# Three PSUM tiles for the attention results, routing constants on GpSimd, and a new instruction order, in an attention and mixture-of-experts kernel

## The chip, the cores and the metric

The kernel runs on one core of a Trainium2 chip. The metric is the device time of one execution in microseconds (us), here the median of several runs. The engines are named as the profile names them: PE is TensorE's matmul, PEld its weight load, DVE is VectorE, ACT is ScalarE, POOL is GpSimd and SP is SyncE, which issues most DMAs.

## The reference

Inputs q, k, v have 8 batches, 8 heads, 576 positions and 64 channels. The first half is attention with a memory:

```
scores = q k^T / 8, causal;  a = softmax(scores);  local = a v
q_p = phi(q),  phi(x) = x + 1 for x > 0, else exp(x)
mem = (q_p M_prev) / (q_p z_prev + 1e-6)
out = sigmoid(beta) * mem + (1 - sigmoid(beta)) * local
```

The second half takes the 4608 positions as tokens x of 512 channels. Logits are x times w_gate, for 8 experts. Pairs of token and expert are taken in the order of falling logits, with at most 576 tokens for an expert. Each expert e then computes relu(x w1[e]) w2[e] for its tokens.

## The kernel before

Values are kept as pairs of 16-bit floats (a high part and a rest), so that the products are nearly of 32-bit accuracy. Attention is done in 16 units of four heads (a unit is half of a batch). For each unit the kernel loads q, k, v and M_prev, splits and transposes them, takes row maxima of the scores, and then, head by head, makes the scores in PSUM (`S`), exponentiates them on ACT into a high part `ph` and a full value, and subtracts the two into a low part `pl` (`P2`: on DVE at line 1339 or on POOL at line 1342, as a letter of the string `p2k` says for each of the 12 pieces of a unit).

With these a head's results are made on PE. A row of queries has five blocks of positions. `AVm` is 10 matmuls that make the five blocks of memory results, `AV1`, `AV2` and `AV3` are 9, 21 and 15 matmuls that make the five blocks of local results. Every result block has 65 columns: 64 channels and the denominator. Each matmul of these is recorded at line 1041, a helper. All blocks of all heads lie in one PSUM tile of three banks:

```
avs=ps.tile([128,3,512],F32,name='avs')
def slot(i): return avs[:,2*b,65*i:65*i+65] if i<7 else avs[:,1,65*(3*b+i-7):65*(3*b+i-6)]
```

`b` is 0 or 1 and alternates from head to head: a head has bank 0 or bank 2 for seven blocks, and three places in bank 1, the middle bank, for the rest. On DVE a head then takes `N0` (two instructions, lines 1385 and 1386, that gather the denominators), `N1` (reciprocal, line 1390), `N2` (line 1389, the memory blocks divided, out of PSUM into the SBUF tile `xt`; two instructions, as the blocks lie in two banks), `N2b` (line 1389, the local blocks divided in place, in PSUM) and `N3` (line 1403, their sum into `xt`). Three of four heads go so; the fourth divides all ten blocks in one step and leaves the sum to POOL. The results are then split into 16-bit pairs (`ncast`, `nsub`), written to DRAM and multiplied with w_gate into logits.

After attention the kernel routes: for each of 8 experts a threshold is searched on DVE, ACT and PE, the tokens' numbers are listed, the rows gathered, and two matrix products run. All but the first expert's routing lies beside the products of the expert before.

The order is planned by a program in the kernel file. Each of its nodes has an engine, or alternatives, a duration, data keys that it reads and writes, pools of buffers that it takes (`acq`) and frees (`rel`), and a due time; a list schedule follows from these. The table `PR` holds the due times' offsets (`off`, `dl`), additions to durations that steer the choice between engines (`bias`), fixed choices by piece (`pin`, where `*` leaves it free) and `p2k`. The planner treats the two halves of `avs` as two independent buffers (`av=2`). The instructions are then issued in that order, and the waits between engines are made from the tiles that the instructions touch.

Constants for routing are made during attention (`route_consts`, lines 1498 to 1506 on DVE, after integer patterns from POOL), and the gate weights are scaled and split at the start (line 1152, three instructions on DVE).

Of the kernel before, what the change touches and what calls it, by code (L numbers as in the profile page):

```python
# [23 lines left out]
          'kba': -30628.42,  # L24
          'kbd': -21514.39,
          'kbv': -30457.33,
          'kha': -9689.05,
          'khp': 68039.52,
          'khv': 14252.18,
          'klp': -32138.21,  # L30
          'klv': -19015.13,
          'mh2a': 18046.34,
          'mh2v': -7557.72,
          'mha': -6556.62,
          'mhv': 118047.29,
          'mlp': -61301.72,
          'mlv': 103205.55,
          'mra': 13094.26,
          'mrv': -49929.19,
          'mza': 13667.92,  # L40
          'mzv': 154718.09,
          'nap': -923.34,
          'nav': -3267.9,
          'nca': -17356.34,
          'ncp': 19952.5,
          'ncv': -19147.84,
          'nsp': -33806.3,
          'nsv': 8700.47,
          'p2p': 3448.83,
          'p2v': -5.41,  # L50
          'p4sp': -99613.75,
          'p4sv': -14317.61,
          'pha': -24715.3,
          'php': 10489.25,
          'phra': -10695.76,
          'phrv': 20287.52,
          'phv': -24278.1,
          'plp': 4297.99,
          'plv': 4879.76,
          'prepca': -46562.05,  # L60
          'prepcv': -134550.89,
          'qha': -51241.95,
          'qhp': 17974.64,
          'qhv': -60171.16,
          'qlp': 26287.18,
          'qlv': 78420.0,
          'qmovea': 42586.74,
          'qmoved': 5914.55,
          'qmovev': -9885.0,
          'tea': -3123.88,  # L70
          'tev': -3783.25,
          'vha': -3050.15,
          'vhp': 15722.78,
          'vhv': 48350.7,
          'vlp': 27996.84,
          'vlv': 29979.61,
          'xtea': -62406.89,
          'xtev': 142184.48},
 'dl': {'0': {'AV': 3.03,
              'MX': -439.58,  # L80
              'N': -45.87,
              'P2': 95.25,
              'S': -79.48,
              'fin1': 396.93,
              'fin2': 87.35,
              'kb': 3.48,
              'kh': -937.23,
              'kl': -795.9,
              'kt': 387.88,
              'lk': -688.72,  # L90
              'lm': -210.42,
              'lq': -541.06,
              'lv': -99.14,
              'maxrem': -157.75,
              'mfin': 328.48,
              'mfin2': -56.76,
              'mfin3': -180.29,
              'mh': -838.83,
              'ml': 193.21,
              'mz': -1034.64,  # L100
              'nadd': -286.28,
              'ncast': 852.81,
              'nsub': -703.35,
              'ph': -141.8,
              'phe': -764.62,
              'phr': -38.36,
              'phs': 62.7,
              'pl': -977.2,
              'prep': 200.37,
              'proc24': 671.37,  # L110
              'pt': 192.37,
              'qh': -404.47,
              'ql': 386.07,
              'qmove': 129.64,
              'qt': -168.61,
              'sj4': -1434.02,
              'vh': 667.29,
              'vl': 490.09},
        '1': {'AV': 58.78,
              'MX': -104.28,  # L120
              'N': -347.1,
              'P2': -339.06,
              'S': 606.52,
              'fin1': 484.59,
              'fin2': 2.45,
              'kb': 126.23,
              'kh': -563.06,
              'kl': 507.8,
              'kt': 591.73,
              'lk': -540.92,  # L130
              'lm': -577.58,
              'lq': -166.76,
              'lv': -66.59,
              'maxrem': 342.62,
              'mfin': -545.34,
              'mfin2': 9.06,
              'mfin3': -80.01,
              'mh': -618.46,
              'ml': 449.29,
              'mz': 14.48,  # L140
              'nadd': -926.32,
              'ncast': -198.57,
              'nsub': 506.43,
              'ph': -560.71,
              'phe': -372.41,
              'phr': -876.37,
              'phs': 209.62,
              'pl': 213.14,
              'prep': 164.36,
              'proc24': 454.72,  # L150
              'pt': 233.41,
              'qh': -427.92,
              'ql': 1274.93,
              'qmove': 1075.02,
              'qt': 47.11,
              'sj4': -45.54,
              'vh': -285.68,
              'vl': -176.11},
        '10': {'AV': 758.58,
               'MX': -73.66,  # L160
               'N': 72.38,
               'P2': 279.63,
               'S': -8.46,
               'fin1': -248.92,
               'fin2': 347.06,
               'kb': 358.91,
               'kh': 442.41,
               'kl': 79.29,
               'kt': -298.24,
               'lk': -767.97,  # L170
               'lm': 14.63,
               'lq': -633.6,
               'lv': 673.6,
               'maxrem': 724.62,
               'mfin': -318.66,
               'mfin2': 386.87,
               'mfin3': 137.35,
               'mh': 981.75,
               'ml': -129.7,
               'mz': 550.95,  # L180
               'nadd': -120.05,
               'ncast': 1.51,
               'nsub': -229.44,
               'ph': 489.25,
               'phe': 997.89,
               'phr': -1284.21,
               'phs': 165.79,
               'pl': -224.45,
               'prep': 191.53,
               'proc24': -144.35,  # L190
               'pt': -242.79,
               'qh': 501.96,
               'ql': 984.38,
               'qmove': -284.76,
               'qt': -711.9,
               'sj4': -187.91,
               'vh': 1156.16,
               'vl': -17.9},
        '11': {'AV': 355.99,
               'MX': -108.14,  # L200
               'N': -177.3,
               'P2': -1118.12,
               'S': 356.14,
               'fin1': 358.76,
               'fin2': 223.29,
               'kb': -146.64,
               'kh': -152.48,
               'kl': 559.23,
               'kt': -15.25,
               'lk': 955.17,  # L210
               'lm': 246.97,
               'lq': 882.81,
               'lv': -420.65,
               'maxrem': 30.53,
               'mfin': -41.22,
               'mfin2': 83.89,
               'mfin3': -400.44,
               'mh': -51.28,
               'ml': -126.76,
               'mz': -129.3,  # L220
               'nadd': 107.08,
               'ncast': -1366.45,
               'nsub': 536.08,
               'ph': -283.95,
               'phe': -649.23,
               'phr': -270.74,
               'phs': -481.4,
               'pl': 292.58,
               'prep': -518.41,
               'proc24': -4.05,  # L230
               'pt': -249.01,
               'qh': 480.34,
               'ql': 615.5,
               'qmove': 459.89,
               'qt': -26.77,
               'sj4': 164.57,
               'vh': -414.34,
               'vl': 21.65},
        '12': {'AV': 167.39,
               'MX': 1.03,  # L240
               'N': 559.11,
               'P2': -154.37,
               'S': -49.69,
               'fin1': 221.57,
               'fin2': 527.79,
               'kb': 1200.71,
               'kh': -74.53,
               'kl': -144.63,
               'kt': -309.14,
               'lk': -221.84,  # L250
               'lm': -263.39,
               'lq': -614.17,
               'lv': 244.4,
               'maxrem': 565.59,
               'mfin': 257.23,
               'mfin2': 16.16,
               'mfin3': 507.27,
               'mh': 215.36,
               'ml': 291.75,
               'mz': 463.51,  # L260
               'nadd': -356.78,
               'ncast': 12.76,
               'nsub': 868.62,
# [631 lines left out]
class Sched:  # L895
# [18 lines left out]
    def run(self,tol=100,sem=170,same=110,t0=0.0,hwg=450,dlat=1300,dend=950,ph=2800.0,thr=3060,pel=60):  # L914
# [20 lines left out]
        def pick(e):  # L935
            C=cand[e]; best=None; L=[]; Q=line[e]
            f=free[e]
            for c in C:
# [7 lines left out]
                elif e=='V' and (x.slack or x.nm in LK) and s<poolb-1: s=poolb-1  # L946
# [11 lines left out]
        while left:  # L958
            b=None
# [931 lines left out]
```

## Time and profile before

| | us |
|---|---|
| median of 3 runs (971.52 to 975.38) | 972.42 |
| profiled execution | 974.23 |
| span of its instructions | 972.40 |
| busy: PE / DVE / POOL / ACT | 814.7 / 717.4 / 599.7 / 578.3 |
| mean granted TensorE clock (1.0 is 2.4 GHz) | 0.947 |

The profiled execution is 1.8 us above the median and its span 1.8 us below its time. Busy time is summed over stages that have different limits, so it is read stage by stage: attention takes about the first 495 us, the routing of the first expert with nothing beside it about 60 us, and the experts the rest.

### The profile page before, as it was taken

What the parts mean: (1) busy time and instruction counts of PE and PEld (TensorE: products, weight loads), DVE (VectorE), ACT (ScalarE), POOL (GpSimd) and SP (SyncE); (2) the same over time, 40 slices, a digit from 0 to 9 for tenths busy, and PEclk for the clock granted to TensorE, in tenths of its full rate; (3) what the DMA queues carried; (4) which work ended last, traced back from release to release, by engine and by line L of the source; (5) the groups of instructions that cost most, each with busy time, mean ns of one, the idle gap of its engine ahead of it and who ended that gap; (6) DMA issues with size and microseconds to landing.
All of it is one profiled execution on the core that took longest, in us unless ns stands there. A gap on an engine that the chain in (4) does not pass through costs nothing.

```text
span 972.4 us, 25309 instructions
## 1 busy us (share of the span) xinstructions
PE 814.7 (84%) x9736; PEld 523.4 (54%) x9736; DVE 717.4 (74%) x2385; ACT 578.3 (59%) x1046; POOL 599.7 (62%) x594
## 2 busy tenths in 40 slices
PE   4587888878888888888831797999999999999995
PEld 3365666656667666767620543445454444444442
DVE  8998889998889899896678977768787777502010
ACT  4475776677587767768622557483838383754110
POOL 7768787889889878968610237382647373585101
PEclk9897999999899999999955699899999999999999
DMA  5566454528555443533411427362737273692101
GB/s 130 117 142 147 111 118 93 128 66 168 115 131 124 92 105 69 118 66 66 94 36 61 162 79 220 127 177 81 231 102 237 94 232 102 216 269 78 38 12 38
DMA packets 230302, 116.49 MB, mean 120 GB/s; under 512 B 199013, under 2 KB 208229, under 8 KB 230181
## 3 DMA queue, kind: packets, MB, share of 16 engines
q1 hardware_dynamic: 224293, 96.00, 39.1%
q0 software_dynamic: 5888, 18.88, 5.8%
q8 instruction: 76, 1.25, 0.5%
q14 instruction: 45, 0.37, 0.1%
HBM read 72.40 MB, written 18.87 MB: 94 GB/s over the span
## 4 chain that ended last, share of the span: by engine, by line
PE 44%; DVE 7%; issue 1%; ACT 1%; DMA 1%; POOL 0%; POOLq 0%; DVEq 0%; ACTq 0%
PE py L1540 19%; PE ph L1540 16%; PE avs L1041 3%; PE prem L1540 2%; DVE scr L1774 2%; PE pr L1540 1%; DMA out_dram<-ys,idx 1%; PE pb L1041 1%; DVE xt L1389 1%; PE pl L1540 1%; DVE avs L1389 1%; DVE xt L1403 0%; DVE th L1781 0%; ACT wh L1689 0%; DVE kk L1780 0%
## 5 line engine op out<-in xcount | busy, mean ns | idle before, releaser
L1690 POOL TENSOR_TENSOR wl<-wst,wh 128x1024 f16<-128x1024 f32 x60 | 127.6, 2150 | 81.9 <-ACT wh L1689 64.7
L1540 PE MATMUL ph<-xT,wh 128*128 128x512 f16 (+1 forms) x560 | 164.0, 368 | 1.7 <-DVE hl L1733 1.0
L1334 ACT ACTIVATE ph<-pb 128x512 f16<-128x512 f32 x192 | 115.7, 602 | 42.5 <-PE pb L1041 32.0
L1197 DVE TENSOR_REDUCE mx<-pb 128x1 f32<-128x512 f32 (+3 forms) x256 | 123.3, 547 | 2.2 <-PE pb L1041 2.0
L1041 PE MATMUL avs<-V,ph 128*128 128x65 f16 x1792 | 103.6, 194 | 24.8 <-DVE xt L1389 11.4
L1752 POOL DMA_INDIRECT out_dram<-ys,idx x40 | 38.7, 968 | 126.3 <-ACT ys L1747 70.9
L1041 PEld LDWEIGHTS <-ph 128*128 128x128 f16 x1792 | 94.3, 99 | 33.4 <-issue 30.3
L1342 POOL TENSOR_TENSOR pl<-pf,ph 128x512 f16<-128x512 f32 x80 | 95.2, 1193 | 19.7 <-ACT pf L1341 18.3
L1041 PE MATMUL pb<-qT,kT 128*128 128x64 f16 (+3 forms) x576 | 102.3, 242 | 6.0 <-DVE mx L1197 2.8
L1540 PEld LDWEIGHTS <-wh 128*128 128x128 f16 x1072 | 68.7, 99 | 59.3 <-issue 3.8
L1041 PE MATMUL avs<-V,pl 128*128 128x65 f16 x896 | 99.5, 197 | 0.0
L1540 PE MATMUL ph<-xT,wl 128*128 128x512 f16 (+1 forms) x280 | 98.8, 367 | 0.0
L1041 PE MATMUL pb<-kT,qM 128*128 128x256 f16 (+5 forms) x384 | 83.9, 314 | 16.9 <-DVE mx L1197 9.4
L1041 PE MATMUL pb<-qM,kB 128*128 128x64 f16 (+3 forms) x576 | 97.1, 241 | 0.1
L1540 PE MATMUL py<-wl,hh 128*128 128x512 f16 x256 | 97.0, 379 | 0.0
L1540 PE MATMUL py<-wh,hh 128*128 128x512 f16 x256 | 97.0, 379 | 0.0
L1540 PE MATMUL prem<-xT,wh 128*128 128x64 f16 x512 | 96.7, 193 | 0.0
L1733 DVE SCALAR_TENSOR_TENSOR hl<-ph,hh 128x512 f16<-128x512 f32 x64 | 44.0, 688 | 65.2 <-ACT hh L1732 64.6
L1774 DVE TENSOR_SCALAR_CACHE_REDUCE scr<-p_LwT,th 128x320 f16<-128x320 f32 x168 | 85.1, 544 | 2.7
L1772 ACT ACTIVATE scs<-p_LwT,th 128x320 f16<-128x320 f32 x84 | 47.0, 560 | 64.8 <-DVE th L1781 50.7
L1041 PEld LDWEIGHTS <-pl 128*128 128x128 f16 x896 | 85.2, 99 | 0.0
L1732 ACT ACTIVATE hh<-ph 128x512 f16<-128x512 f32 x64 | 37.9, 594 | 74.9 <-PE ph L1540 49.6
(289 smaller groups left out, 2293.1 us busy)
## 6 DMA issues: line engine op xcount, KB each, us to landing
wst<-in_moe_w_dram SPq DMA_DIRECT2D x32, 1024.0 KB
kf<-in_k_dram SPq DMA_DIRECT2D x64, 128.0 KB
qf<-in_q_dram SPq DMA_DIRECT2D x64, 128.0 KB
vf<-in_v_dram SPq DMA_DIRECT2D x64, 128.0 KB
xd<-xs SPq DMA_DIRECT2D x16, 512.0 KB
kB<-kT SPq DMA_DIRECT2D x15, 288.0 KB
kf<-in_k_dram SPq DMA_DIRECT2D x32, 32.0 KB
qf<-in_q_dram SPq DMA_DIRECT2D x32, 32.0 KB
```

Of the source, the lines that this page charges most:

```text
L1041: def MM(*a,**kw): mm(*a,skip_group_check=True,**kw)
L1197: R=lambda o,i: nc.vector.tensor_reduce(o,i,axis=mybir.AxisListType.X,op=ALU.max)
L1334: c=SC.add('Eh',[('A',478)],lambda x,a=a: nc.scalar.activation(phs_[x.buf['ph']][:,0:512],pbb[a.buf['pb']],AF.Exp,scale=0.125),acq=('ph',) ...
L1342: e=SC.add('P2',[('P',1113)],lambda x,c=c,d=d: nc.gpsimd.tensor_sub(pls_[c.buf['ph']][:,0:512],pfs[d.buf['pf']],phs_[c.buf['ph']][:,0:512] ...
L1389: MU=lambda o,i,d: nc.vector.tensor_tensor(o,i,d,op=ALU.mult)
L1540: def MM(*a,**kw): mm(*a,skip_group_check=True,**kw)
L1690: SC.add('sp',[('P',2079)],lambda x,ws=ws,k=k,s=s: G_.tensor_sub(wl[:,k,s],ws(),wh[:,k,s]),r=[key+('h',)],w=[key+('l',)],after=[b],rel=rel ...
L1732: b=SC.add('hh',[('A',478)],lambda x,a0=a0,f=f: A_.activation(hh[:,f],phb[a0.buf['ph']],AF.Relu),w=[('hh',f)],after=[y],prio=pr('hh',n,pos ...
L1733: SC.add('hl',[('V',602)],lambda x,a0=a0,f=f: V_.scalar_tensor_tensor(hl[:,f],phb[a0.buf['ph']],0.0,hh[:,f],op0=ALU.max,op1=ALU.subtract), ...
L1752: z=SC.add('scat',[('P',655 if i<4 else 330,'p',0,(1034,'n'))],lambda x,e=e,i=i,r_=r_: G_.indirect_dma_start(out=out,out_offset=bass.Indir ...
L1772: SC.add('sign',[('A',547)],lambda x,j=j,t_=t_,c_=c_: A_.activation(scs[j-KV],LwT,AF.Sign,bias=t_[:,4:5],accum_out=c_[:,j:j+1]),r=['LwT',( ...
L1774: V(462,lambda x,j=j,t_=t_,c_=c_: V_.tensor_scalar(scr[j],LwT,t_[:,j+1:j+2],0.0,op0=ALU.is_ge,op1=ALU.add,accum_out=c_[:,j:j+1]),r=['LwT', ...
```

## The change

The tile `avs` becomes three tiles of one bank each: `avo0` and `avo1`, which alternate from head to head and hold the five local blocks, and `avm`, which holds the five memory blocks of whichever head is in work (pool `am=1`). `AVm` moves behind `AV3`, and `N0` waits for both. In heads of the first kind `N2` is one instruction and frees `avm`; the local bank is freed by `N3`. The gate weights and most routing constants are made by POOL; two integer operations stay on DVE. The numbers of `PR` are new throughout, `p2k` has one more `v` (8 instead of 7 of 12 pieces on DVE), `pin` leaves more pieces free (`te` is the copy of transposed pieces out of PSUM, nine to a unit: k, q and phi(q) by three), and the planner's two uses of `poolb-1` become `poolb+1`. The table `PM` of the expert stage is the same.

```
- 'p2k': 'vpvpvvpvpvpv',
+ 'p2k': 'vpvpvvvvpvpv',
...
-         'te': 'v*vvv*av*a**',
+         'te': '**v*vva**avv',
...
- 'run': {'tol': 19.5},
+ 'run': {'tol': 13.3},
...
-    avs=ps.tile([128,3,512],F32,name='avs')
+    avo=[ps.tile([128,512],F32,name=f'avo{i}') for i in range(2)]; avm=ps.tile([128,512],F32,name='avm')
...
-    SC=Sched(dict(pb=5,av=2,ph=NP,...
+    SC=Sched(dict(pb=5,av=2,am=1,ph=NP,...
...
-        nc.vector.tensor_scalar(wf,wf,64.0,...); nc.vector.tensor_copy(wgs[:,:,0:8],wf); nc.vector.tensor_sub(...)
-    one('wgs',[('V',500)],f,-40,r=['wf'],w=['wgs'])
+        nc.gpsimd.tensor_scalar(wf,wf,64.0,...); nc.gpsimd.tensor_copy(wgs[:,:,0:8],wf); nc.gpsimd.tensor_sub(...)
+    one('wgs',[('P',500)],f,-40,r=['wf'],w=['wgs'])
...
-                        o=slot(i+5)
+                        o=avm[:,65*i:65*i+65]
...
-                        o=slot(i)
+                        o=avo[(box[0] or x).buf['av']][:,65*i:65*i+65]
...
-            a0=SC.add('AVm',[('T',300)],...,acq=('av',),after=ch('A'),prio=pr('AV',u,3*j)); box[0]=a0; ch('A',a0)
-            a1=SC.add('AV1',[('T',279)],...,after=[a0]+ce,prio=pr('AV',u,3*j+.1))
+            a1=SC.add('AV1',[('T',279)],...,acq=('av',),after=ch('A')+ce,prio=pr('AV',u,3*j+.1)); box[0]=a1
...
+            a0=SC.add('AVm',[('T',300)],...,acq=('am',),after=ch('Am')+[a3],prio=pr('AV',u,3*j+.4)); ch('Am',a0)
...
-            n0=SC.add('N0',[('V',158)],f,r=['gt'],w=[('de',di)],after=[a3],prio=pr('N',u,3*j))
+            n0=SC.add('N0',[('V',158)],f,r=['gt'],w=[('de',di)],after=[a3,a0],prio=pr('N',u,3*j))
...
-                def f(x): t=xts[x.buf['xt']][:,0]; MU(t[:,0:2],own(5,7)[:,:,0:64],dv(5,7)); MU(t[:,2:5],mid()[:,:,0:64],dv(7,10))
-                n2=SC.add('N2',[('V',476)],f,...,acq=('xt',),prio=pr('N',u,3*j+.2))
+                def f(x): MU(xts[x.buf['xt']][:,0],mem()[:,:,0:64],dv(5,10))
+                n2=SC.add('N2',[('V',402)],f,...,acq=('xt',),rel=[('am',a0)],prio=pr('N',u,3*j+.2))
...
+    out.append(('V',75,lambda: V_.tensor_scalar(it[:,9:10],it[:,8:9],7,None,op0=ALU.bitwise_and)))
+    out.append(('V',140,lambda: V_.tensor_scalar(i2,i2,7,None,op0=ALU.bitwise_and)))
...
-        V_.tensor_copy(EW,it[:,0:8]); V_.tensor_copy(s5,it[:,16:21]); ...
-    out.append(('V',600,f))
+        G_.tensor_copy(EW,it[:,0:8]); G_.tensor_copy(s5,it[:,16:21]); G_.tensor_copy(pcode,it[:,9:10]); G_.tensor_scalar(pcode,...)
+    out.append(('P',900,f))
+    def f(): G_.tensor_copy(fl,i2); G_.tensor_scalar(blk,fl,0.0,None,op0=ALU.is_equal)
+    out.append(('P',560,f))
...
+        G_.tensor_scalar(tri,jp,...); G_.tensor_scalar(triI,jp,...); G_.memset(ones,1.0)
+    out.append(('P',550,f))
+    out.append(('P',750,lambda: G_.tensor_copy(sio,i5)))
```

## Rows read from the trace of the kernel before

**Rows 1.** Busy time by stretch of the span: the stretch and its length, then for PE, PEld, DVE, ACT and POOL the busy us and the count of instructions, then the granted TensorE clock, the DMA share and GB/s. The first three cut the span into attention, routing and experts, the others cut attention.
```profile
0.00:495.00 495.00, 392.95 (x6890) 313.51 (x6890) 429.24 (x1135) 340.66 (x636) 393.10 (x452) 0.96 0.50 109
495.00:555.00 60.00, 21.54 (x210) 16.79 (x211) 51.58 (x260) 18.57 (x44) 6.88 (x8) 0.53 0.28 100
555.00:972.00 417.00, 400.16 (x2640) 193.06 (x2637) 236.58 (x993) 219.04 (x366) 199.75 (x135) 0.99 0.43 136
...
30.00:495.00 465.00, 377.86 (x6759) 302.64 (x6758) 404.24 (x1068) 328.94 (x616) 369.07 (x386) 0.96 0.49 107
30.00:440.00 410.00, 335.97 (x5832) 266.40 (x5832) 367.77 (x949) 292.39 (x542) 332.83 (x346) 0.96 0.51 111
440.00:495.00 55.00, 41.90 (x931) 36.23 (x928) 36.47 (x119) 36.55 (x75) 36.23 (x41) 0.95 0.38 76
30.00:100.00 70.00, 51.28 (x724) 38.35 (x724) 64.32 (x142) 43.32 (x77) 52.07 (x47) 0.88 0.61 136
```
**Rows 2.** The waits of DVE from 20 to 495 us: who waited for whom, us in total, times, longest.
```profile
DVE avs L1389 <- PE avs L1041: 14.9, 19, 1.8
DVE de L1385 <- PE avs L1041: 10.0, 17, 1.3
DVE xt L1389 <- PE avs L1041: 9.4, 18, 1.8
DVE xt L1403 <- PE avs L1041: 7.6, 13, 0.9
```
**Rows 3.** The waits of PE from 20 to 495 us on DVE's work on the tile `avs`, same columns.
```profile
PE avs L1041 <- DVE xt L1389: 17.3, 30, 1.9
...
PE avs L1041 <- DVE avs L1389: 9.4, 15, 1.8
PE avs L1041 <- DVE xt L1403: 9.0, 15, 2.3
...
PE avs L1041 <- DVE de L1386: 3.3, 9, 0.8
```
**Rows 4.** From the chain of work that ended last, asked for 440 to 449 us: start, us, what.
```profile
440.13 0.32 PE avs L1041 x10
...
440.48 0.17 DVE de L1385
...
441.77 0.57 DVE xt L1389 x2
...
442.36 0.51 DVE avs L1389
...
442.91 0.82 PE avs L1041 x21
...
443.76 0.50 DVE xt L1403
...
444.30 0.94 PE avs L1041 x25
```
**Rows 5.** The waits of PE from 440 to 495 us, same columns as rows 3.
```profile
PE avs L1041 <- DVE xt L1389: 4.4, 7, 1.4
PE avs L1041 <- DVE avs L1389: 3.4, 6, 1.0
PE avs L1041 <- DVE xt L1403: 2.2, 4, 0.7
PE avs L1041 <- DVE de L1386: 0.5, 2, 0.2
```
**Rows 6.** DVE's busy time of single lines during attention (columns as rows 1, DVE alone): in this order line 1152, 1498, 1500, 1504 and 1506; and, after the dots, one instruction of line 1500 (min, median and max ns, start).
```profile
0.00:495.00 495.00, 5.44 (x3) 0.96 0.50 109
0.00:495.00 495.00, 1.32 (x5) 0.96 0.50 109
0.00:495.00 495.00, 3.18 (x3) 0.96 0.50 109
0.00:495.00 495.00, 1.19 (x3) 0.96 0.50 109
0.00:495.00 495.00, 0.83 (x1) 0.96 0.50 109
...
L1500 DVE TENSOR_SCALAR it<-it x1: 775/775/775, 154.9 to 154.9; 128x128 int32<-128x128 int32 x1
```
**Rows 7.** The instructions of DVE, and after the dots those of POOL, in order of time near 32 us: start, us, what.
```profile
32.22 3.16 DVE L1152 TENSOR_TENSOR wgs<-wf,wgs 128x32 f16<-128x32 f32 x1
...
32.11 0.67 POOL L1277 TENSOR_TENSOR ml<-mf,mh 64x260 f16<-64x260 f32 x1
32.75 2.58 POOL L1286 TENSOR_TENSOR V<-vf,V 128x512 f16<-128x512 f32 x2
```
**Rows 8.** Groups of instructions by line and shape during attention, on DVE and after the dots on POOL: count, busy us, mean ns, and the idle time before them.
```profile
L1339 DVE TENSOR_TENSOR pl<-pb,ph 128x512 f16<-128x512 f32 x112 | 76.0, 681 | 4.4 <-ACT pb L1338 3.6 <-issue 0.6
...
L1389 DVE TENSOR_TENSOR avs<-avs,de 128x320 f32<-128x320 f32 x48 | 23.8, 496 | 15.5 <-PE avs L1041 14.9
...
L1084 DVE COPY kT<-pb 128x1024 f16<-128x1024 f16 x29 | 19.5, 681 | 0.6 <-PE pb L1183 0.4
...
L1085 POOL TENSOR_SCALAR xs<-xt 128x320 f16<-128x320 f32 x30 | 13.7, 460 | 16.2 <-DVE xt L1403 15.1 <-DVE p_mxb L1447 1.1
```

More of the change, by code (lines that the diff above doesn't have):

```diff
@@ L41 @@
-          'mzv': 154718.09,
+          'kba': -38256.38,
+          'kbd': -26666.66,
+          'kbv': -40060.57,
+          'kha': 14508.09,
+          'khp': 79231.15,
+          'khv': 24617.63,
+          'klp': -1086.28,
+          'klv': 16564.27,
+          'mh2a': 20115.95,
+          'mh2v': -71452.4,
+          'mha': 22820.34,
+          'mhv': 89368.52,
+          'mlp': -31325.33,
+          'mlv': 98087.6,
+          'mra': 17856.1,
+          'mrv': -40742.45,
+          'mza': 48409.13,
@@ L42 @@
+          'mzv': 168176.88,
           'nap': -923.34,
           'nav': -3267.9,
[L44 to L48, printed above, removed]
+          'nca': -18457.66,
+          'ncp': 25373.91,
+          'ncv': -21886.13,
+          'nsp': -32165.33,
+          'nsv': -132.24,
           'p2p': 3448.83,
           'p2v': -5.41,
-          'p4sp': -99613.75,
-          'p4sv': -14317.61,
-          'pha': -24715.3,
@@ new lines @@
+          'p4sp': -101839.76,
+          'p4sv': 7041.96,
+          'pha': -31945.75,
+          'php': 29271.45,
+          'phra': -17422.93,
+          'phrv': 21464.53,
+          'phv': -15662.98,
+          'plp': -19639.54,
+          'plv': 43456.26,
+          'prepca': -6518.9,
+          'prepcv': -117462.96,
+          'qha': -48927.36,
+          'qhp': 53729.35,
+          'qhv': -70868.4,
+          'qlp': 66042.22,
+          'qlv': 67290.35,
+          'qmovea': 37764.26,
+          'qmoved': 9935.43,
@@ L722 @@
  'npf': 4,
- 'off': {'AV': 177.53,
-         'MX': -21.07,
-         'N': 7.33,
-         'P2': -141.04,
-         'S': 16.64,
-         'fin1': 439.29,
-         'fin2': 31.35,
-         'kb': -11.42,
-         'kh': -970.56,
-         'kl': -510.97,
-         'kt': -34.62,
-         'lk': 55.72,
-         'lm': 43.56,
-         'lq': 4.98,
-         'lv': -18.77,
-         'maxrem': -6.07,
-         'mfin': 358.34,
-         'mfin2': -411.47,
-         'mfin3': -1198.57,
-         'mh': 363.54,
-         'ml': -675.04,
-         'mz': 1535.38,
-         'nadd': 156.85,
-         'ncast': 399.45,
-         'nsub': 690.37,
-         'ph': 208.86,
-         'phe': 668.92,
-         'phr': 1636.46,
-         'phs': 299.77,
-         'pl': 1404.7,
-         'prep': -1028.29,
-         'proc24': 1243.97,
-         'pt': -21.68,
-         'qh': -138.07,
-         'ql': -1516.77,
-         'qmove': -323.14,
-         'qt': -253.2,
-         'sj4': -196.03,
-         'vh': -383.85,
-         'vl': -494.26},
- 'p2k': 'vpvpvvpvpvpv',
- 'pin': {'kb': 'd*va',
-         'kh': '*',
+ 'off': {'AV': 354.36,
+         'MX': -71.76,
+         'N': 35.4,
+         'P2': -404.5,
+         'S': 79.95,
+         'fin1': 1411.67,
+         'fin2': 45.35,
+         'kb': -155.13,
+         'kh': -864.76,
+         'kl': -325.66,
+         'kt': -45.19,
+         'lk': 36.12,
+         'lm': 5.45,
+         'lq': 24.59,
+         'lv': -52.41,
+         'maxrem': 69.93,
+         'mfin': 533.74,
+         'mfin2': -740.97,
+         'mfin3': -1009.04,
+         'mh': 367.78,
+         'ml': -815.85,
+         'mz': 581.35,
+         'nadd': 89.93,
+         'ncast': 229.29,
+         'nsub': 716.8,
+         'ph': -250.69,
+         'phe': 1029.76,
+         'phr': 1761.5,
+         'phs': 219.4,
+         'pl': 1360.18,
+         'prep': -1283.21,
+         'proc24': 1390.48,
+         'pt': 95.92,
+         'qh': -614.21,
+         'ql': -1858.34,
+         'qmove': -829.71,
+         'qt': -301.43,
+         'sj4': -153.0,
+         'vh': -344.36,
+         'vl': -365.2},
+ 'p2k': 'vpvpvvvvpvpv',
+ 'pin': {'kb': 'd*ad',
+         'kh': 'a',
          'kl': '*pp',
@@ L945, in pick @@
                     if s<lockV and c[1][-1].__class__ is not tuple: s=lockV
-                elif e=='V' and (x.slack or x.nm in LK) and s<poolb-1: s=poolb-1
+                elif e=='V' and (x.slack or x.nm in LK) and s<poolb+1: s=poolb+1
                 if len(x.alts)>1:
@@ L951, in pick @@
                     for a in x.alts:
-                        if a is not c[1] and max(free[a[0]],t,poolb-1 if a[0]=='V' and x.nm in LK else 0)+bi(a)<mine: worse=True; break
+                        if a is not c[1] and max(free[a[0]],t,poolb+1 if a[0]=='V' and x.nm in LK else 0)+bi(a)<mine: worse=True; break
                     if worse: continue
@@ L1352, in avp @@
             def avp(x,part):
-                b=(box[0] or x).buf['av']
-                def slot(i): return avs[:,2*b,65*i:65*i+65] if i<7 else avs[:,1,65*(3*b+i-7):65*(3*b+i-6)]
                 if part==0:
@@ L1375, in outs @@
             ce=[x for p in B_ for x in p]
-            a0=SC.add('AVm',[('T',300)],wg=650,fn=lambda x: avp(x,0),r=rm_,acq=('av',),after=ch('A'),prio=pr('AV',u,3*j)); box[0]=a0; ch('A',a0)
-            a1=SC.add('AV1',[('T',279)],wg=585,fn=lambda x: avp(x,1),r=rv,after=[a0]+ce,prio=pr('AV',u,3*j+.1))
+            a1=SC.add('AV1',[('T',279)],wg=585,fn=lambda x: avp(x,1),r=rv,acq=('av',),after=ch('A')+ce,prio=pr('AV',u,3*j+.1)); box[0]=a1
             a2=SC.add('AV2',[('T',647)],wg=1365,fn=lambda x: avp(x,2),r=rv,after=[a1],prio=pr('AV',u,3*j+.2))
-            a3=SC.add('AV3',[('T',465)],wg=877,fn=lambda x: avp(x,3),r=rv+[('p4l',U2,x) for x in range(h2,2)]+[('p4h',U2,x) for x in range(h2,2)],after=[a2],rel=[('ph',c) for c,e in B_],prio=pr('AV',u,3*j+.3))
-            bi=lambda: a0.buf['av']
-            own=lambda a,b: avs[:,2*bi(),65*a:65*b].rearrange('p (i e) -> p i e',e=65)
-            mid=lambda: avs[:,1,195*bi():195*bi()+195].rearrange('p (i e) -> p i e',e=65)
+            a3=SC.add('AV3',[('T',465)],wg=877,fn=lambda x: avp(x,3),r=rv+[('p4l',U2,x) for x in range(h2,2)]+[('p4h',U2,x) for x in range(h2,2)],after=[a2],rel=[('ph',c) for c,e in B_],prio=pr('AV',u,3*j+.3)); ch('A',a3)
+            a0=SC.add('AVm',[('T',300)],wg=650,fn=lambda x: avp(x,0),r=rm_,acq=('am',),after=ch('Am')+[a3],prio=pr('AV',u,3*j+.4)); ch('Am',a0)
+            own=lambda a,b: avo[a1.buf['av']][:,65*a:65*b].rearrange('p (i e) -> p i e',e=65)
+            mem=lambda: avm[:,0:325].rearrange('p (i e) -> p i e',e=65)
             di=(4*u+j)%2; de=des[di].rearrange('p k i -> p (k i)'); eg=lambda a,b: eps[:,g,a:b]
             def f(x):
-                nc.vector.scalar_tensor_tensor(de[:,0:7],own(0,7)[:,:,64],1.0/256,eg(0,7),op0=ALU.mult,op1=ALU.add)
-                nc.vector.scalar_tensor_tensor(de[:,7:10],mid()[:,:,64],1.0/256,eg(7,10),op0=ALU.mult,op1=ALU.add)
-            n0=SC.add('N0',[('V',158)],f,r=['gt'],w=[('de',di)],after=[a3],prio=pr('N',u,3*j))
+                nc.vector.scalar_tensor_tensor(de[:,0:5],own(0,5)[:,:,64],1.0/256,eg(0,5),op0=ALU.mult,op1=ALU.add)
+                nc.vector.scalar_tensor_tensor(de[:,5:10],mem()[:,:,64],1.0/256,eg(5,10),op0=ALU.mult,op1=ALU.add)
+            n0=SC.add('N0',[('V',158)],f,r=['gt'],w=[('de',di)],after=[a3,a0],prio=pr('N',u,3*j))
             dv=lambda a,b: de[:,a:b,None].to_broadcast([128,b-a,64])
```

1370 lines of the change are left out of this document (667 added, 703 removed).

## The prediction

> **What bounds the kernel now.** I read first the table of busy time by stretch [rows 1]. The expert stage (417 us) has PE busy for 400.2 us, and neither its code nor its table of numbers is touched; the 60 us of routing before it are a chain that the change doesn't touch either. So the change can only move the end of attention, now near 495 us, and what follows moves with it one for one. In attention DVE is the busiest engine: 404.2 of the 465 us from 30 to 495 us. PE (377.9), POOL (369.1) and ACT (328.9) have more room. DVE is busy for 367.8 of 410 us (0.897) up to 440 us, but in the last 55 us only for 36.5 (0.66), with PE at 41.9 (0.76): there no engine is full.
>
> Then I read what ended DVE's idle time [rows 2]. Of its 61 us (465 - 404.2) nearly all of 41.9 us (14.9 + 10.0 + 9.4 + 7.6) went by until PE had done something on `avs`. PE in turn waited 39.0 us (17.3 + 9.4 + 9.0 + 3.3) for DVE's work on `avs` [rows 3]. Each waits for the other on one tile, and the chain shows how [rows 4]. `N2b` runs from 442.36 to 442.87, then PE's 21 matmuls (`AV2` of the next head) from 442.91, then `N3` at 443.76, then 25 matmuls (`AV3` and `AVm`) at 444.30: the two take strict turns. By the data they needn't. `N2b` and `N3` need only results that `N0` has waited for already, and `AV2` writes the other head's bank. Even `N0` at 440.48 follows the ten matmuls of an `AVm`, although a head's `AVm` comes first and its `AV3` last in this order, so these ten belong to the next head. Waits on `N2b` and `N3`, which touch no middle bank, show that the exclusion goes by the whole tile of three banks, not by bank. The planner counts two independent buffers there and doesn't see this.
>
> The Trainium skill's page "PSUM — Partial Sum Buffer" (section "PSUM bank collisions raise a hardware error") says that software has to keep two engines apart on one bank and quadrant, while different banks run clean together. By that rule the turns in the middle bank were needed and those between bank 0 and bank 2 not; the trace has both, so most of the measured turns aren't the chip's demand. The rule also speaks against a part of the change: all heads' memory results in one bank must be kept apart head by head, which is the third rival below.
>
> **The change part by part.**
>
> *Three tiles.* With one tile to a bank, `AV1` to `AV3` of a head no longer meet `N2b` and `N3` of the head before. All of 14.9 + 9.4 + 7.6 = 31.9 us of DVE's waits (`N2b`, `N2`, `N3`) are false, for these run behind their own `N0`; of `N0`'s 10.0 us a part is the true wait for the last matmul [rows 2]. What is late next? If nothing, DVE up to 440 us would be as dense as it is now outside these waits: 404.2 / (465 - 41.9) = 0.955. If other waits take their place at once it stays at 0.897. Between these stands a measured stretch, 30 to 100 us, with 64.3 of 70 us, or 0.919 [rows 1]. I take 0.919, since its work is of the same kind, queues with in-order issue will still leave holes, and the full 0.955 would need every wait of DVE to vanish without a successor.
>
> *DVE's own work.* Constants: lines 1152, 1498, 1500, 1504 and 1506 hold 5.44 + 1.32 + 3.18 + 1.19 + 0.83 = 11.96 us of DVE [rows 6]. Two integer operations stay: 0.78 us and, of line 1498, about a fifth, 0.26. So 10.9 us go. `N2` in 48 heads becomes one instruction: the pair takes 0.57 us, one of 320 columns 0.51 [rows 4], so 48 x 0.06 = 2.9 us go. `p2k` brings one more subtraction per unit to DVE: 16 x 0.68 = 10.9 us come [rows 8]. The letters of `te` leave three more wide copies per unit free, 45 in all. Of the wide k copies, whose second is free before, DVE still made 29 of 30 [rows 8], so I let 1 in 15 leave DVE: 3 x 0.68 = 2.0 us (bounds 0 and 45 x 0.68 = 31; the row decides). The sum is -10.9 - 2.9 + 10.9 - 2.0 = -4.9 us.
>
> *POOL.* It takes 13 small instructions, each at most about the 0.46 us of its 320-column scaling [rows 8], so at most 6.0 us, against sixteen 512-column subtractions that leave it. It isn't the bound; I take no cost for its own time. Beside DVE it is another matter: DVE's 128x32 subtraction took 3.16 us and ended at 35.38, just as POOL's run of 32.11 to 35.33 did [rows 7], so one held the other. The same can happen the other way round with the moved work: 0 to 6.0 us for DVE. I take 0, as POOL has less work in sum, and keep 6.0 in the range. The Trainium skill's page "SBUF — State Buffer" (section "SBUF: two separate sides") says that the ports which DVE and GpSimd share are an exclusive lock, held for the whole instruction, so that the other engine fully blocks. Rows 7 agree; by that rule the moved work would give its whole length back to DVE, and the sum below would be 956 and not 950.
>
> *`AVm` behind `AV3`, one `avm`.* PE's instructions are the same in number. New is that `AVm` of a head waits for `N2` of the head before, and behind it in PE's queue stand the next scores and transposes, for which ACT and DVE wait. A head has 465 / 64 = 7.3 us; from the end of its matmuls to the end of `N2` go 441.77 + 0.57 - 440.45 = 1.9 us [rows 4]. The wait is over long before, at nothing, as long as DVE isn't 5 us behind.
>
> *SP's queue, due times, `pin`.* The loads, the copies by DMA and the transposes are the same in number; only their places change. The bound is the density above in both directions.
>
> *The sum up to 440 us.* DVE has 367.8 - 4.9 = 362.9 us to do. At 0.919 that is 394.9 us, 15.1 less than 410; at 0.955 380.0 (30.0 less); at 0.897 404.6 (5.4 less).
>
> *The last 55 us.* Here PE waited 10.5 us (4.4 + 3.4 + 2.2 + 0.5) for DVE on `avs` [rows 5] and the turns are the chain [rows 4]. PE's 41.9 us of work are the floor, so 0 to 13.1 us can go. I take two thirds of the 10.5: 7 us, since true waits (the last head's `N` after its `AVm`) stay.
>
> *Together* -15.1 - 7 = -22.1 us against the profiled 974.2: 952.1. The median lies 1.8 us below the profiled execution, so 950.3; I say 950. The bounds are -30.0 - 13.1 = -43.1 (929) and -5.4 (967).
>
> **The rivals.**
>
> *The turns stay, in other clothes.* The waits on `avs` become waits on the next thing (maxima, subtractions, scores), density stays 0.897 and only the work removed counts: 974.2 - 5.4 - 1.8 = 967. For it: in 410 us DVE was at 0.897 already, so a tenth is all there is. Against it: the turns end both engines' waits at once, DVE's 41.9 and PE's 39.0.
>
> *Given back elsewhere.* The new order costs in loads, in POOL's chain (`P2`, `nsub`) or in the hand-over to routing what the tiles gain: 972. For it: POOL is at 369 of 465 us [rows 1] and its results end the heads. Against it: POOL loses work.
>
> *One memory bank is too few, slower.* DVE's queue puts `N2` late, `AVm` of the next head stands at the front of PE's queue, and scores, exponentials and subtractions behind it starve. Now the waits on `N2` cost PE 17.3 us in 30 times, 0.58 each and at the longest 1.9 [rows 3]. At 1.0 for each of 64 heads DVE would idle 64 us in place of 41.9, so +22.1 - 5.4: 974.2 + 16.7 - 1.8 = 989. It decides from the point at which DVE is more than about 5 us behind a head's matmuls. Against it: it has to happen in every head, with 7.3 us for each.
>
> **How the numbers follow.** About 0.5% (5 us) is what a measurement of this kernel can tell from no change. The forecast has 0.72, the first rival 0.13, the second 0.05, the slower one 0.10. Of the first rival's 967, which sits on the border of 967.6, I give 0.08 to faster and 0.05 to no change. Faster is 0.72 + 0.08 = 0.80, no change 0.05 + 0.05 = 0.10, slower 0.10. The likeliest case alone spans 929 to 967. The range for 8 in 10 runs from 928 to 968: it leaves out the second rival and the slower one (0.15) and some 0.05 of the likeliest at its ends.
>
> **What would show it.** In the profile after, `N2b` and `N3` should wait for PE hardly at all, DVE's waits on the attention matmuls should fall from 41.9 us to under 15, all of them at `N0`, and PE's waits for `N2b` and `N3` to nearly nothing; PE's waits at `AVm` for `N2` stay under 10 us. DVE from 30 to 440 us should be near 0.92, its work some 5 us less, and the first routing step some 22 us earlier, with routing and experts as long as before. The prediction is wrong if DVE's density stays at 0.90, if PE waits at `AVm`, or if the stages behind attention change in length.

## The result, and the profile after

The changed kernel takes 939.84 us (median of 4 runs, 938.76 to 940.85) beside 972.72 for the kernel before: a ratio of 0.9658, 95% interval [0.9635, 0.9681]. The profiled execution took 938.76 us with a span of 937.0. The forecast was 950: 22 us less were expected and 33 came.

The waits first. These are all of DVE's and PE's waits for each other over the attention results, in the changed kernel from 20 to 460 us: who waited for whom, us in total, times, longest. They answer to [rows 2] and [rows 3].

```profile
DVE de L1383 <- PE avm L1041: 1.4, 4, 0.5
...
DVE de L1382 <- PE avo L1041: 0.7, 2, 0.4
...
PE avo L1041 <- DVE xt L1400: 1.3, 1, 1.3
```

41.9 us of DVE's waiting have become 2.1, and 39.0 of PE's have become 1.3. `N2b` and `N3` wait for nothing any more; what is left is at `N0`, where the data needs it. What DVE now waits for most is the exponential that it subtracts, 9.0 us where 3.6 stood in [rows 8], and PE waits for DVE's maxima and subtractions. No wait of PE at `AVm` for `N2` is listed:

```profile
DVE pl L1339 <- ACT pb L1338: 9.0, 17, 1.6
DVE mx L1197 <- PE pb L1041: 2.5, 5, 0.9
...
PE pb L1041 <- DVE mx L1197: 11.9, 32, 1.3
PE pb L1183 <- DVE pl L1339: 6.1, 4, 4.6
```

The busy time by stretch (columns as in [rows 1]) in the changed kernel: attention up to the first step of the threshold search, then all the rest; after the dots from 30 us to that step, and the last 60 us of it; after the next dots two stretches in the middle.

```profile
0.00:459.70 459.70, 390.45 (x6927) 313.86 (x6927) 422.35 (x1115) 341.91 (x642) 381.12 (x453) 0.95 0.55 118
459.70:937.00 477.30, 420.75 (x2809) 207.38 (x2809) 292.01 (x1219) 237.38 (x409) 204.55 (x140) 0.94 0.41 130
...
30.00:459.70 429.70, 373.12 (x6796) 301.46 (x6796) 398.09 (x1052) 330.58 (x625) 357.43 (x385) 0.95 0.55 117
399.70:459.70 60.00, 50.15 (x1084) 42.57 (x1082) 48.67 (x159) 45.12 (x95) 43.06 (x50) 0.93 0.40 80
...
200.00:300.00 100.00, 91.50 (x1721) 74.25 (x1719) 96.48 (x257) 79.66 (x150) 91.79 (x93) 1.00 0.60 132
300.00:400.00 100.00, 91.12 (x1701) 74.22 (x1699) 96.08 (x248) 79.76 (x152) 82.96 (x84) 0.98 0.53 106
```

The same for the kernel before, cut at its own first threshold step:

```profile
0.00:503.70 503.70, 396.41 (x6927) 316.02 (x6927) 435.30 (x1168) 341.35 (x637) 395.03 (x454) 0.96 0.50 108
503.70:972.40 468.70, 418.25 (x2809) 207.34 (x2809) 282.10 (x1219) 236.92 (x409) 204.70 (x140) 0.94 0.41 133
...
30.00:503.70 473.70, 381.32 (x6796) 305.15 (x6795) 410.30 (x1101) 329.63 (x617) 371.00 (x388) 0.95 0.49 106
443.70:503.70 60.00, 42.03 (x904) 36.11 (x902) 40.32 (x144) 33.87 (x71) 35.91 (x41) 0.88 0.33 72
```

The first threshold step comes at 459.7 us in place of 503.7, so attention is 44.0 us shorter, twice what was forecast. But from that step to the end the changed kernel takes 477.3 us where the kernel before took 468.7: 8.6 us are given back in a stage that the prediction called untouched. The rows give the 44.0 in parts. From 30 us to the first step DVE's work fell from 410.3 to 398.1 us, 12.2 less. Its idle time in the last 60 us fell from 19.7 (60 - 40.3) to 11.3 (60 - 48.7), 8.4 less. Ahead of them it fell from 43.7 (473.7 - 60 - 410.3 + 40.3) to 20.3 (429.7 - 60 - 398.1 + 48.7), 23.4 less. So DVE was busy for 349.4 of 369.7 us there (0.945) in place of 370.0 of 413.7 (0.894), and from 200 to 400 us for 192.6 of 200 (0.963).

### The profile page after: what moved, and what is told of

It reads as the page before. It is cut to its first block, busy times and chain, and to the rows that moved or that the text cites. A ratio compares the mean times of both kernels' runs of the same rounds, so it can differ in the third digit from the quotient of the medians.

```text
span 937.0 us, 25227 instructions
## 1 busy us (share of the span) xinstructions
PE 811.2 (87%) x9736; PEld 521.2 (56%) x9736; DVE 714.4 (76%) x2333; ACT 579.3 (62%) x1051; POOL 585.7 (63%) x593
## 4 chain that ended last, share of the span: by engine, by line
PE 54%; DVE 21%; ACT 8%; POOL 6%; issue 5%; DMA 5%; SPq 1%; POOLq 0%; DVEq 0%; ACTq 0%
PE py L1539 20%; PE ph L1539 17%; PE pb L1041 7%; DVE mx L1197 5%; PE avo L1041 4%; DVE scr L1773 2%; PE prem L1539 2%; DVE pl L1339 2%; DMA xT<-xs 2%; ACT ph L1334 2%; PE pb L1183 2%; POOL h L1174 1%; ACT pb L1338 1%; PE pr L1539 1%; DVE xt L1386 1%
## 5 line engine op out<-in xcount | busy, mean ns | idle before, releaser
L1041 PE MATMUL avo<-V,ph 128*128 128x65 f16 x1792 | 102.9, 195 | 1.5 <-DVE xt L1400 1.3
L1041 PE MATMUL avo<-V,pl 128*128 128x65 f16 x896 | 98.7, 198 | 1.3 <-POOL pl L1342 1.3
L1339 DVE TENSOR_TENSOR pl<-pb,ph 128x512 f16<-128x512 f32 x128 | 86.4, 678 | 9.6 <-ACT pb L1338 9.0
L1342 POOL TENSOR_TENSOR pl<-pf,ph 128x512 f16<-128x512 f32 x64 | 75.5, 1181 | 22.2 <-ACT pf L1341 22.2
```

Of the source, the lines that this page charges most:

```text
L1041: def MM(*a,**kw): mm(*a,skip_group_check=True,**kw)
L1339: e=SC.add('P2v',[('V',602)],lambda x,a=a,c=c: nc.vector.tensor_sub(pls_[c.buf['ph']][:,0:512],pbb[a.buf['pb']],phs_[c.buf['ph']][:,0:512] ...
L1342: e=SC.add('P2',[('P',1113)],lambda x,c=c,d=d: nc.gpsimd.tensor_sub(pls_[c.buf['ph']][:,0:512],pfs[d.buf['pf']],phs_[c.buf['ph']][:,0:512] ...
```

## The experiments

Each experiment takes one part of the change, or puts one part back. Times are medians. The kernel before was measured again beside each group, with medians of 976.29 us (e1, e2, e4, e5), 974.53 (e6 to e9) and 971.91 (e3, e10), and the ratios of the experiments are to these; so medians of different groups can be compared only to within some 4 us. "First step" is the start of the threshold search in the profiled execution, "rest" what its span holds behind that. The two columns come from one execution each, which can lie some us from the median: for e9 the span is 930.3 and the median 938.24.

| kernel | first step | rest | median us | ratio to before, 95% interval |
|---|---|---|---|---|
| before | 503.7 | 468.7 | 972.72 | 1 |
| after | 459.7 | 477.3 | 939.84 | 0.9658 [0.9635, 0.9681] |
| e1, before with three tiles | 468.9 | 468.8 | 939.70 | 0.9624 [0.9585, 0.9663] |
| e2, after with one tile | 498.7 | 477.9 | 978.26 | 1.0028 [1.0005, 1.0051] |
| e10, before with two tiles | 495.2 | 466.8 | 963.35 | 0.9923 [0.9892, 0.9953] |
| e4, before, constants on GpSimd, planned anew | 510.1 | 469.2 | 982.01 | 1.0080 [1.0053, 1.0108] |
| e5, after, constants on DVE, planned anew | 478.7 | 474.6 | 957.51 | 0.9821 [0.9783, 0.9859] |
| e8, after, constants on DVE, order kept | 463.0 | 472.9 | 938.32 | 0.9661 [0.9611, 0.9711] |
| e9, e1, constants on GpSimd, order kept | 463.2 | 467.1 | 938.24 | 0.9653 [0.9610, 0.9695] |
| e3, after with all tables of before | 478.1 | 465.3 | 942.92 | 0.9694 [0.9661, 0.9727] |
| e7, before, experts in the new order | 502.8 | 476.1 | 980.14 | 1.0056 [1.0030, 1.0081] |
| e6, after, experts in the old order | 460.2 | 466.6 | 928.96 | 0.9551 [0.9500, 0.9601] |

**e1: the tiles alone.** Every block stays where it was, also in the middle bank that two heads share, and in the two traces every engine has the same instructions in the same order. The slices that DVE reads are rewritten like `slot`.

```
-    avs=ps.tile([128,3,512],F32,name='avs')
+    avs=[ps.tile([128,512],F32,name=f'avs{i}') for i in range(3)]
...
-                def slot(i): return avs[:,2*b,65*i:65*i+65] if i<7 else avs[:,1,...]
+                def slot(i): return avs[2*b][:,65*i:65*i+65] if i<7 else avs[1][:,...]
...
```

> The kernel before, with its three banks as three tiles and nothing else: same places for every block (the middle bank still shared by two heads), same order, same tables. If the exclusion by the whole tile is what cost the time (my theory): DVE's waits in N2b and N3 for the attention matmuls fall from 22.5 us to under 5, the first threshold step (503.7 us in the kernel before, 459.7 in the changed one) comes 18 to 30 us earlier, and the time is 943 to 955 us. If the new order and tables made the gain (rival): within 5 us of 972, since order and tables are the old ones.

First step 468.9, 34.8 us earlier, and 939.7 us: more than the theory's 18 to 30 and below its 943 to 955, and the rival is out. Three tiles under the old order make the time as short as the whole change does. Of DVE's 41.9 us of waits on the attention results 5.6 are left, nearly all at `N0` (lines 1385 and 1386), and none at `N2b` or `N3`. Of PE's 39.0 us 8.2 are left, 3.3 of them at `N2`, so the middle bank that two heads still share costs little. DVE's waits from 20 to 469 us, the five longest, and after the dots all of PE's on these tiles:

```profile
DVE pl L1339 <- ACT pb L1338: 6.3, 11, 1.4
DVE mx L1197 <- PE pb L1041: 4.9, 9, 1.4
DVE de L1385 <- PE avs L1041: 4.2, 9, 1.0
DVE xs L1084 <- POOL xt L1397: 4.0, 1, 4.0
DVE lt L1437 <- PE pb L1041: 1.6, 3, 0.7
...
PE avs L1041 <- DVE xt L1403: 4.9, 6, 2.2
PE avs L1041 <- DVE xt L1389: 3.3, 6, 0.9
```

**e2: one tile again, under the new order.**

```
-    avo=[ps.tile([128,512],F32,name=f'avo{i}') for i in range(2)]; avm=ps.tile([128,512],F32,name='avm')
+    avs=ps.tile([128,3,512],F32,name='avs'); avo=[avs[:,0],avs[:,2]]; avm=avs[:,1]
```

> The changed kernel with its three banks as parts of one tile again, same order otherwise. Theory: PE and DVE take turns again, waits of both on the tile over 60 us together, the first threshold step later by 25 us or more, time 962 to 985 us, since this order was planned without the turns. Rival (order and tables made the gain): 940 to 948 us.

978.3 us, and the gain is gone: of attention's 44.0 us 5.0 are left (503.7 to 498.7), and the longer stage behind it (477.9) takes them. The waits came back: DVE's on the tile, from 20 to 499 us, and from the chain of waits (start, us, what) the turns as in [rows 4]:

```profile
DVE de L1382 <- PE avs L1041: 14.5, 26, 1.7
DVE avs L1386 <- PE avs L1041: 9.6, 16, 1.1
DVE xt L1400 <- PE avs L1041: 7.3, 11, 1.9
...
DVE xt L1386 <- PE avs L1041: 4.9, 12, 0.7
```

```profile
439.98 0.50 DVE xt L1400
...
440.52 1.41 PE avs L1041 x40
...
441.96 0.16 DVE de L1382
...
442.55 0.50 DVE xt L1386
...
443.07 0.51 DVE avs L1386
...
443.61 0.50 DVE xt L1400
```

No bank is shared between a head's `N2b` and the next head's `AV1` to `AV3` here, and still DVE waits 9.6 us before `N2b` and 7.3 before `N3`. All of DVE's waits on the tile are 36.3 us and PE's for DVE's work on it 31.0, 67.3 together.

**e10: is it the bank or the tile?** Two tiles: the two own banks as halves of one, the middle bank by itself.

```
-    avs=ps.tile([128,3,512],F32,name='avs')
+    avs=ps.tile([128,2,512],F32,name='avs'); avd=ps.tile([128,512],F32,name='avd')
```

> The kernel before with two tiles: the two heads' own banks are the two halves of one tile, the middle bank is a tile of its own. No two heads share a bank of the first tile. If the exclusion goes by the tile: N2b and N3 of one head still take turns with the next head's matmuls in the other bank, DVE's waits in them stay at 12 us or more of 22.5, first threshold step at 490 to 504 us, time 958 to 973. If it goes by bank: as with three tiles, first step near 469 us, time 938 to 945 us.

It goes by the tile. In the first tile no two heads share a bank, but the turns go on. DVE's waits, 20 to 492 us:

```profile
DVE avs L1389 <- PE avs L1041: 12.2, 19, 1.4
DVE xt L1389 <- PE avs L1041: 8.0, 16, 1.9
DVE xt L1403 <- PE avs L1041: 7.7, 13, 1.0
DVE de L1385 <- PE avs L1041: 6.8, 15, 1.1
```

`N2b` and `N3` hold 19.9 us of waits beside 22.5 in the kernel before. To free the middle bank gains 8.5 us of attention (503.7 to 495.2), to part the two own banks another 26.3 (495.2 to 468.9).

**e4 and e5: the constants, with the planner free.** e4 puts the new lines for gate weights and constants into the kernel before, e5 the old ones into the changed kernel; the edit of one line of e4:

```
-    one('wgs',[('V',500)],f,-40,r=['wf'],w=['wgs'])
+    one('wgs',[('P',500)],f,-40,r=['wf'],w=['wgs'])
```

> The kernel before with the gate weights and routing constants made by GpSimd, nothing else by hand (the planner places them anew). DVE's work falls by some 11 us. If DVE's work is the bound one for one (rival): 961 us. Theory: while the turns on the tile last, work taken from DVE becomes waiting on the tile, so only a part comes out: 965 to 972 us.

> The changed kernel with the gate weights and routing constants made by DVE again. Without the turns DVE is busy 95 % of the time, so the 11 us should come back nearly one for one: 946 to 951 us by the theory that DVE is now the bound; 938 to 943 us if another engine is.

Both missed. e4 is slower than the kernel before beside it, 982.0 against 976.3 us, though DVE has less to do (430.9 us in attention in place of 435.3); e5 loses 18 us by the medians and 16 by the ratios, more than the 11 us of work that return. In both the planner made another order from the same tables, so they don't tell the constants from the order. That led to two runs in which the order is kept and only the engine of these instructions is another.

**e8 and e9: the constants, in place.** In e8 the planner still counts the instructions as GpSimd's, but they are emitted for DVE; e9 does the reverse in e1. One line of e8:

```
-    out.append(('P',750,lambda: G_.tensor_copy(sio,i5)))
+    out.append(('P',750,lambda: V_.tensor_copy(sio,i5)))
```

> The changed kernel, its order exactly as planned, but the gate weights and routing constants emitted for DVE at the places planned for GpSimd. The run with the planner free cost 19 us of attention, more than DVE's 11 us of work. If that work itself costs one for one: first threshold step at 469 to 472 us, time 949 to 952. If the planner's other order made most of the 19 us: first step at 461 to 466, time 941 to 946 us.

> The kernel before with three tiles and, at the places planned for DVE, the gate weights and routing constants emitted for GpSimd. With the tiles alone the first threshold step came at 468.9 us. If DVE is the bound once the turns are gone, 11 us less of its work bring it to 458 to 462 us and the time to 927 to 932 us, so that tiles and constants together hold the whole gain of attention. If the new order is what is left (9 us of attention between the tiles alone and the changed kernel): 466 to 469 us, 936 to 940 us.

e8 takes 938.3 us and its first step is at 463.0; e9 takes 938.2 us and its first step is at 463.2. By the profiled executions the constants are worth 3 to 6 us of attention (463.0 against 459.7 and 468.9 against 463.2), by the medians nothing that can be told (938.3 against 939.8, and 938.2 against 939.7). So most of what e5 lost was the other order, as e8's second reading said (its first step lies within that reading's 461 to 466, its time below its 941 to 946). e9's first step fell between its two readings, and its time within the second's.

**e7 and e6: the 8.6 us behind attention.** Marks of one step per expert (the `relu` of the last 64 tokens, on ACT) show that one expert's period is longer in the changed kernel: from the third to the fourth mark 59.5 us, where the kernel before has 51.2. The order of both stages comes from the same planner code, and its `poolb-1` had become `poolb+1` for both. Both runs make the number an argument; e7 gives +1 to the experts of the kernel before, e6 gives -1 to those of the changed kernel. From e6:

```
-    def run(self,...,thr=3060,pel=60):
+    def run(self,...,thr=3060,pel=60,pbx=1):
...
-                elif e=='V' and (x.slack or x.nm in LK) and s<poolb+1: s=poolb+1
+                elif e=='V' and (x.slack or x.nm in LK) and s<poolb+pbx: s=poolb+pbx
...
-    for x in SC.run(ph=P_.get('ph',5000.0),**P_.get('run',{})): x.fn(x)
+    for x in SC.run(ph=P_.get('ph',5000.0),pbx=-1,**P_.get('run',{})): x.fn(x)
```

> The kernel before, with +1 in place of -1 in the planner of the expert stage alone. If the number makes the loss: the third expert takes 57 to 60 us and the time rises by 7 to 10 us over the kernel before (979 to 983 beside 972). If it was a matter of when attention ends: unchanged.

> The changed kernel, with the planner's number in the expert stage put back from +1 to -1, so that this stage has the order of the kernel before; attention as in the changed kernel. From the first threshold step to the end the kernel before took 468.7 us and the changed one 477.3; the third expert took 59.5 us in place of 51.2. If the planner's new number did that: 468 to 469 us behind a first step at 460, so 929 to 932 us. If it is chance or a matter of when attention ends: 938 to 941 us.

Both went as the planner's number has it. e7 loses 5.6 us against the kernel before beside it (980.1 against 974.5; 7 to 10 were expected) and its rest grows to 476.1; e6's rest is 466.6, and its 928.96 us beat both kernels. In the table the five kernels with the new order of the experts have rests of 472.9 to 477.9, the seven with the old one 465.3 to 469.2. In the changed kernel the longer expert shows PE idle and then slow. First its period and, after the dots, the same of the kernel before (columns as in [rows 1]); then, in the changed kernel, what PE waited for in it, and in e7:

```profile
643.60:703.10 59.50, 54.77 (x347) 25.48 (x346) 40.20 (x167) 28.10 (x53) 24.48 (x17) 0.94 0.45 133
...
687.70:738.90 51.20, 51.20 (x345) 24.89 (x344) 39.37 (x173) 33.03 (x59) 29.18 (x21) 1.00 0.51 167
```

```profile
PE pr L1539 <- DVE scr L1773: 4.7, 3, 2.2
...
PE ph L1540 <- DMA xT<-xg: 2.8, 1, 2.8
```

So 4.7 of the 8.3 us (59.5 - 51.2) are idle time of PE, and 3.6 are longer work. From the chain of waits of the changed kernel (start, us, what), and from its busy time at 5 us a row:

```profile
657.90 1.96 PE py L1539 x9
...
664.89 1.03 DVE scr L1773 x4
666.15 3.63 PE py L1539 x9
```

```profile
655.00:660.00 5.00, 5.00 (x30) 2.44 (x29) 3.08 (x14) 1.31 (x4) 3.78 (x5) 1.00 0.53 165
660.00:665.00 5.00, 3.80 (x19) 1.52 (x17) 2.04 (x12) 1.20 (x4) 2.26 (x3) 1.00 0.85 211
665.00:670.00 5.00, 4.04 (x13) 1.55 (x14) 2.75 (x15) 1.86 (x5) 0.10 (x1) 0.66 1.23 209
```

Nine matmuls take 1.96 us at 657.9 and 3.63 at 666.15, after PE had stood idle until the threshold search on DVE (`scr`) was done. The granted clock is 1.00 up to 665 us (2.4 GHz) and 0.66 in the 5 us after, so part of them ran at the lower level, 1.2 GHz. The late instruction isn't the same in every kernel with this order: in the changed kernel PE waits 4.7 us for the search, in e7 2.8 us for the transfer of the gathered rows (`xT<-xg`) and 0.6 for the search. The runs show that the order makes the loss; why the one or the other comes late stays open.

**e3: the old tables under the new structure.** All numbers of `PR` and both planner numbers as in the kernel before.

> The changed kernel with all tables and both planner numbers of the kernel before: three tiles with one for the memory results, constants on GpSimd, one instruction for N2; experts in the old order. If structure makes the gain and the new tables add little: first threshold step at 460 to 470 us, time 928 to 938 us. If the tables have to fit the structure (as two runs with a free planner suggest, where moving the constants cost 6 and 19 us): 470 to 480 us, time 938 to 948.

The second reading holds: first step 478.1, 942.9 us. With this structure the new tables, and the planner's number for attention with them, are worth 17.9 us of attention (478.1 to 460.2 in e6, whose experts are in the same order), 1.4 % in the ratios.

## Why the prediction was right, and where not

**The turns on one tile: right.** Waits on `N2b` and `N3` were called false, and they went with the tiles alone (e1), came back with one tile (e2), and go by the tile and not by the bank (e10). Of the prediction's own signs the waits came as stated, the density, the work and the first step moved further than stated, and one sign of being wrong came true: the stages behind attention changed in length.

**The size: the term that failed is the density of 0.919.** The prediction took DVE up to 440 us to be as dense (busy for as large a share) as in 30 to 100 us, because "queues with in-order issue will still leave holes", and kept 0.955 as the end of the range. At 0.919 DVE's idle time there would have been 32.0 us (394.9 - 362.9) where 42.2 (410 - 367.8) stood: 10.2 of the forecast 22.1 us. In its place 23.4 went, at a density of 0.945. The false waits left almost without successors; the largest one is DVE's waits for the exponentials, 5.4 us more.

**The last 55 us: right.** 7 us were expected to go; in the last 60 us DVE's idle time fell by 8.4.

**DVE's own work: -4.9 us were expected, -12.2 came** (-13.0 from the start of the span, 435.3 to 422.4). The terms by line: the subtractions came at 10.4 (75.97 to 86.39) where 10.9 were expected, the constants went at 11.6 where 10.9 were, line 1389, now 1386, fell by 4.7 where 2.9 were, the copies by 2.4 where 2.0 were. Other lines moved that had no term: two subtractions of line 1174 (2.9 us) went from DVE to POOL in the new order, lines 1509 and 1514, now 1508 and 1513, took 0.9 us in place of 3.3 with the same instructions, and line 1266, the same 15 instructions, rose by 5.9 us (below). All lines together changed by -9.4. The other 3.6 us are how rows are counted: they overlap at their ends (a 0.68 us instruction is followed by the next after 0.60), rows of different lines by 45.7 us in sum before and 49.2 after, and busy time counts such a stretch once.

**The constants: priced at 10.9 us of DVE, worth 3 to 6 of attention.** Half of the price was not work. In e8 the same instructions took 5.5 us of DVE (3.08 + 0.44 + 0.45 + 1.09 + 0.47); the subtraction of line 1152 took 1.02 us there and 3.16 before, so its length went with its place in the order. And work moved to GpSimd comes back in part. In e9 the lines of the constants hold 11.1 us less of DVE than in e1, but line 1266, which the edit doesn't touch, holds 24.6 in place of 17.3, and DVE's busy time in attention falls only from 430.3 to 427.1. For this the prediction took 0, "as POOL has less work in sum", with 6.0 in its range, though the 13 instructions take no more of POOL than it said (4.9 us of at most 6.0). The Trainium skill's "SBUF — State Buffer" (section "SBUF: two separate sides") says that the ports which the two engines share are locked for a whole instruction. That one engine so holds the other is borne out by line 1266; the loss of the prediction's 956 us is not, as e9 is no slower than e1.

**"Neither its code nor its table of numbers is touched", of the experts: wrong.** The planner is shared, and the prediction read its ±1 as a detail of attention. It costs 8.6 us in the profiled execution. So that the total came near the forecast is partly luck, two errors of opposite sign: attention 22 us better than forecast, experts 9 us worse. Without the second one the time is e6's 928.96, at the lower end of the range.

**One memory bank: no wait at all.** The slower rival needed a wait of 1.0 us at each of the 64 `AVm`, and the profile shows none. What single `avm` gains over the shared middle bank wasn't tried by itself.

**The new order.** With the tiles and the old order (e1) attention is 34.8 us shorter, with everything new 44.0, and with everything new but the tiles (e2) 5.0. So the tiles are worth 34.8 to 39.0 us, and the rest 5.0 to 9.2. That rest is shared by the constants, the merged `N2`, `AVm`'s place and the tables, and the runs don't part these further: e9 takes up 5.7 of it in one execution. What they show is that the tables fit one structure: with the old tables the new structure (e3) is 17.9 us of attention behind the new tables, and 9.2 behind the old structure with three tiles (478.1 against 468.9).

## What to carry to other kernels

When two engines wait for each other over one buffer in strict turns, ask whether the data wants it or the way the buffer is declared: parts of one tile were kept apart as a whole, even in different banks, and to make three tiles of one, with its slices rewritten to match, gained 3.8 % with nothing else changed. Before an edit to a shared planner or helper is called local, list every stage that calls it, and compare the stages behind the edit by their own length: here a gain of 44 us hid a loss of 9. To price one moved piece of work, keep the order and change only its engine, or the new order is measured with it.

## What the runs showed of the hardware

A DVE instruction can take several times its length beside GpSimd's work. The gate weights' subtraction of 128x32, 3.16 us on DVE in [rows 7], takes 1.02 us on DVE at its place in e8, and 0.25 us on POOL in the changed kernel. And DVE's 1152-column scaling at line 1266 went from 1.08 to 1.48 us in the mean, with no change to it; the group before and, after the dots, in the changed kernel (columns as in [rows 8]):

```profile
L1266 DVE TENSOR_SCALAR ef<-qf 128x1152 f32<-128x1152 f32 x15 | 16.2, 1083 | 0.4 <-POOL p L1174 0.3
...
L1266 DVE TENSOR_SCALAR ef<-qf 128x1152 f32<-128x1152 f32 x15 | 22.2, 1478 | 0.3 <-POOL p L1174 0.3
```

The mean hides that the median stays (0.82 and 0.83 us) and that two of the fifteen make the difference: they take 4.26 and 5.05 us, where the longest before took 2.45. The one of 5.05 us in the changed kernel (start, us, engine, what):

```profile
172.51 0.78 POOL L1402 TENSOR_TENSOR xs<-xt,xs 128x320 f16<-128x320 f32 x1
172.58 5.05 DVE L1266 TENSOR_SCALAR ef<-qf 128x1152 f32<-128x1152 f32 x1 [0.28 <-POOL p L1174]
173.26 1.15 POOL L1342 TENSOR_TENSOR pl<-pf,ph 128x512 f16<-128x512 f32 x1
174.38 0.78 POOL L1402 TENSOR_TENSOR xs<-xt,xs 128x320 f16<-128x320 f32 x1
175.12 1.14 POOL L1342 TENSOR_TENSOR pl<-pf,ph 128x512 f16<-128x512 f32 x1
176.23 0.78 POOL L1402 TENSOR_TENSOR xs<-xt,xs 128x320 f16<-128x320 f32 x1
```

It began 0.07 us after the first of five instructions of GpSimd that follow each other without a gap, and ended at 177.63, 0.62 us after the last of them. The same instruction takes 7.75 us in e9, beside eight without a gap, one of them a moved constant, and ends 0.61 us after the last. Where DVE's began first (at 300.58 us) it took its 0.75 us, and GpSimd's subtraction beside it 1.73 in place of 1.15. So what this line costs goes by which engine starts first and by how long GpSimd then runs without a gap, and neither could be read from the busy shares. With DVE at 0.95 the 5.9 us are of the size of the other terms.
